# Moving a handful of vector pieces by half a step to two steps in a software-pipelined FFT-mixing and SiLU kernel

## Chip, cores and metric

One core of a Trainium2 chip. The metric is the device time of one execution in microseconds (us); medians of several runs are given. Engines are named as in the profile: PE is TensorE, PEld its weight loads, DVE is VectorE, ACT is ScalarE, POOL is GpSimd, SP is the engine whose queue issues most transfers.

## The reference

```python
def _attn_ref(x, filt_r, filt_i):            # x: 8 x 3008 x 256
    X = np.fft.rfft(x, axis=1)
    F = (filt_r + 1j * filt_i)[None, :, :]
    return np.fft.irfft(X * F, n=x.shape[1], axis=1).astype(np.float32)

def _moe_ref(x, w_in, w_out):                # x: 24064 x 256, d_ff 2048
    h = x @ w_in
    g = h * (1.0 / (1.0 + np.exp(-h)))
    return (g @ w_out).astype(np.float32)
```

The second function is applied to the result of the first, its 8 batches joined to 24064 rows.

## The kernel before

The FFT of a batch is done as small matrix products in stages ("spectral" work: `sums`, `stage1`, `forward`, `multiply`, `add`, `inverse`, `stage3`). The two large products with SiLU between them use a two-by-two block scheme with 7 products in place of 8 (`hidden`, `project`). A batch takes 48 steps of the large products, one pair of token blocks every 8 steps; while batch b runs, the spectral work of batch b+1 is slipped between its products. A step has 8 rounds. Every spectral piece is put at a step and a round, and all pieces are emitted in that order, so their place in each engine's program is fixed by hand (excerpts; "..." marks cuts, the notes behind # are added):

```python
def put(step, rnd, piece, *args):
    pending.append((step + rnd / ROUNDS, len(pending), lambda: piece(*args)))

def plan(b, part):
    at = STEPS * b                                       # STEPS = 48
    put(at - 49, 0, part["load_x"], 0)
    put(at - 49, 0, part["load_x"], 1)
    for u in range(8):
        put(at + u - 48, 5, part["sums"], u)
        put(at + u - 47, 3, part["stage1"], u)
    ...
    for g in range(NG):                                  # NG = 6 groups
        put(at + 3 * g - 37, 3, part["forward"], g)
        put(at + 3 * g - 37, 5, part["multiply"], g, 0)
        put(at + 3 * g - 36, 1, part["multiply"], g, 1)
        put(at + 3 * g - 36, 5, part["add"], g, 0)
        put(at + 3 * g - 35, 1, part["add"], g, 1)
        put(at + 3 * g - 35, 3, part["inverse"], g)
    put(at - 18, 5, part["load_t4"], 0)
    for g, step in enumerate((-16, -12, -8, -4)):        # stage3: waits for the t4 loads
        ...

stores = (((10, 1), (10, 5)), ((19, 5), (20, 1)), ((28, 5), (29, 1)), ((34, 1), (34, 5)),
          ((42, 1), (42, 5)), ((50, 1), (51, 1)))
for pair in range(len(pairs)):
    pending.append((NJP * pair - 2 + (5 if pair % per == 3 else 1) / ROUNDS, 100,
                    lambda pair=pair: tokens(pair)))
    for chunk in range(2):
        step, rnd = stores[pair % per][chunk]
        pending.append((pair // per * STEPS + step + rnd / ROUNDS, 99 + chunk,
                        lambda pair=pair, chunk=chunk: output(pair, chunk)))
pending.sort(key=lambda p: p[:2])
```

The second entry of a pending piece breaks ties, the smaller one first: a spectral piece has its number in the list, an output chunk 99 or 100.

The part of a step that the spectral pieces must not disturb (`pyz` is a bank of PSUM, the memory that the matmuls here write to, with one buffer; `combine` an elementwise operation):

```python
mm(xo, A11, yt[:, 0, 0:n], True)                         # round 0
...
mm(zo, A12, yt[:, 1, 0:n], True)                         # round 1: overwrites pyz
combine(v, g[:, 0, 0:n], zo, sums[:, 0, 0:n], ALU.add)
finish()                                                 # two subtractions of the step before
...
combine(v, g[:, 2, 0:n], yo, sums[:, 2, 0:n], ALU.add)   # round 4
...
mm(yo, S4, yt[:, 1, n:2 * n], False)                     # round 7: adds to pyz
combine(v, g[:, 1, 0:n], yo, sums[:, 1, 0:n], ALU.add)   # the last read of pyz
```

VectorE's other work: `sums` adds and subtracts two halves of an x tile, `multiply` and `add` are the complex product with the filter, `tokens` forms three differences for a new pair, `drain` copies accumulators out every 8 steps, `output` transposes results before they are stored. POOL adds up the drained blocks (s<-s).

## Time and profile before

| | before |
|---|---|
| runs, us | 2782.37, 2777.46, 2782.92; with three later ones, median 2780.23 |
| PE busy | 96% of 2777.8 us |
| DVE, ACT, POOL busy | 60%, 40%, 18% |
| one batch of 48 steps, steady | 331.24 us |
| PE's waits for DVE's g, as listed | 11.1 us, 17 times |

How to read it: PE is the bound, so what counts is not how busy VectorE is but whether it hands over in time. All losses below are taken from the starts of successive matmuls (0.216 us apart for one record of 256 columns), since the profile models their ends. A step is timed from the start of its round-0 product to that of the next step.

### The profile page before, as it was taken

To read this page: it belongs to the slowest core of one execution; us is meant where nothing else is said; L and a number is where in the kernel's file an instruction comes from. 1 tells how busy PE (TensorE), PEld (TensorE's weight loads), DVE (VectorE), ACT (ScalarE), POOL (GpSimd) and SP (SyncE) were. 2 spreads that over 40 slices of the span, in tenths; PEclk is the share of its full clock that TensorE was granted. 3 is DMA by queue.
4 is the path that set the end of the run, shared out by engine and by line. 5 is a ranking of instruction groups with operands and counts; after the bars stand their busy time and mean duration, and the time that the engine had idled before them with its cause. 6 is when DMAs were issued, how large, how long until landed. Compare 5 with 4: busy or idle time off the path is not lost.

```text
span 2777.8 us, 39564 instructions
## 1 busy us (share of the span) xinstructions
PE 2670.7 (96%) x14592; PEld 2253.3 (81%) x14592; DVE 1657.2 (60%) x3492; ACT 1098.0 (40%) x2994; POOL 505.1 (18%) x738
## 2 busy tenths in 40 slices
PE   3599999999999999999999999999999999999998
PEld 0368889788887888888897888978888788898987
DVE  3676655666556665566656665566655666555555
ACT  1244344433444334443444434443344433444443
POOL 2531310211111111111211121022111211010100
PEclk9799999999999999999999999999999999999999
DMA  9643211321114220232112311133111421110000
GB/s 188 182 121 74 54 40 30 94 71 39 46 39 104 61 51 20 71 84 65 35 38 76 80 47 42 37 82 84 39 46 31 105 63 44 31 25 22 9 15 15
DMA packets 186849, 166.56 MB, mean 60 GB/s; under 512 B 121120, under 2 KB 154528, under 8 KB 186400
## 3 DMA queue, kind: packets, MB, share of 16 engines
q1 hardware_dynamic: 164856, 111.90, 16.9%
q0 software_dynamic: 16256, 47.20, 6.8%
q10 hardware_dynamic: 5544, 4.93, 0.8%
q8 instruction: 114, 1.87, 0.3%
q14 instruction: 79, 0.65, 0.1%
HBM read 88.97 MB, written 74.97 MB: 59 GB/s over the span
## 4 chain that ended last, share of the span: by engine, by line
PE 91%; DVE 4%; DMA 3%; ACT 1%; issue 1%; POOL 0%; ACTq 0%; SPq 0%; DVEq 0%; POOLq 0%
PE acc L491 39%; PE px L435 24%; PE pyz L435 17%; PE pd L355 4%; PE pc L332 3%; PE pa L279 2%; PE pb L302 2%; DMA d<-t 1%; DVE g L406 1%; DVE u L267 1%; DMA t<-d 1%; DMA x<-in_x_dram 0%; DVE z L323 0%; DMA raw<-in_moe_w_out_dram 0%; DVE z L322 0%
## 5 line engine op out<-in xcount | busy, mean ns | idle before, releaser
L491 PE MATMUL acc<-g,w_t 128*128 128x256 f32 (+1 forms) x5376 | 1512.2, 375 | 0.4 <-DVE g L406 0.4
L491 PEld LDWEIGHTS acc<-g,w_t 128*128 128x128 f32 x5376 | 1021.8, 190 | 115.2 <-DVE g L406 0.8
L406 DVE TENSOR_TENSOR g<-pyz,abc 128x256 f32<-128x256 f32 (+1 forms) x1152 | 479.1, 416 | 609.9 <-ACT abc L456 351.9
L406 DVE TENSOR_TENSOR g<-g 128x256 f32<-128x256 f32 (+3 forms) x1152 | 612.4, 532 | 196.6 <-ACT g L439 183.5
L435 PE MATMUL px<-ty,w_t 128*128 128x256 f32 (+1 forms) x2304 | 693.8, 383 | 3.9 <-ACT abc L450 3.3
L439 ACT ACTIVATE g<-g 128x256 f32<-128x256 f32 (+1 forms) x1152 | 472.8, 410 | 243.1 <-DVE g L406 240.6
L435 PEld LDWEIGHTS px<-ty,w_t 128*128 128x128 f32 x2304 | 418.8, 190 | 130.3 <-issue 71.0
L435 PE MATMUL pyz<-y,w_t 128*128 128x256 f32 (+1 forms) x1536 | 454.4, 377 | 11.2 <-DVE g L406 11.1
L406 POOL TENSOR_TENSOR s<-s 128x256 f32<-128x256 f32 (+1 forms) x329 | 265.7, 825 | 1040.4 <-DVE s L509 520.1
L435 PEld LDWEIGHTS pyz<-y,w_t 128*128 128x128 f32 x1536 | 282.1, 189 | 58.1 <-DVE g L406 21.1
L450 ACT COPY abc<-px 128x256 f32<-128x256 f32 (+1 forms) x384 | 141.3, 368 | 373.9 <-PE px L435 373.9
L439 ACT ACTIVATE g<-px 128x256 f32<-128x256 f32 (+1 forms) x384 | 145.9, 380 | 300.8 <-PE px L435 300.8
L456 ACT COPY abc<-px 128x256 f32<-128x256 f32 (+1 forms) x384 | 142.8, 372 | 284.7 <-PE px L435 284.4
L340 POOL DMA_DIRECT2D d<-q x168 | 99.3, 597 | 728.1 <-DVE q L209 720.3
L435 PE MATMUL pyz<-ty,w_t 128*128 128x256 f32 (+1 forms) x768 | 226.4, 377 | 0.0
L435 PE MATMUL px<-y,w_t 128*128 128x256 f32 (+1 forms) x768 | 225.8, 376 | 0.0
L435 PEld LDWEIGHTS pyz<-ty,w_t 128*128 128x128 f32 x768 | 145.2, 190 | 18.8 <-DVE g L406 2.7
L435 PEld LDWEIGHTS px<-y,w_t 128*128 128x128 f32 x768 | 144.6, 190 | 18.1 <-ACT g L439 0.4
L355 PEld LDWEIGHTS pd<-wi_t,t 96*128 96x128 f32 x1024 | 130.6, 201 | 16.6 <-issue 13.9
L355 PE MATMUL pd<-wi_t,t 96*128 96x94 f32 x1024 | 129.5, 283 | 13.0 <-DMA t<-d 13.0
L443 ACT COPY abc<-px 128x256 f32<-128x256 f32 (+1 forms) x384 | 134.1, 349 | 0.1
L284 POOL DMA_DIRECT2D d<-t x128 | 65.5, 516 | 329.7 <-ACT abc L456 283.7
(49 smaller groups left out, 1320.0 us busy)
## 6 DMA issues: line engine op xcount, KB each, us to landing
d<-t POOLq DMA_DIRECT2D x128, 192.0 KB, 3.1
t<-d SPq DMA_DIRECT2D x96, 256.0 KB, 4.1
t<-d SPq DMA_DIRECT2D x64, 384.0 KB, 4.3
d<-q POOLq DMA_DIRECT2D x168, 128.0 KB, 2.7
out_dram<-o SPq DMA_DIRECT2D x636, 32.0 KB, 1.8
x<-in_x_dram SPq DMA_DIRECT2D x120, 128.0 KB, 3.1
x<-in_x_dram SPq DMA_DIRECT2D x120, 60.0 KB, 2.9
raw<-in_moe_w_in_dram SPq DMA_DIRECT2D x16, 256.0 KB, 5.3
```

The source lines that it names most:

```text
L279: nc.tensor.matmul(out=ps[h][64 * par:64 * par + 64], lhsT=wf_t[rows, par], rhs=ut[rows, par], start=True, stop=True)
L284: nc.gpsimd.dma_start(out=d1[par].rearrange("s p n c -> (s p) n c")[:, 4 * u:4 * u + 4, :], in_=t1[64 * par:64 * par + 2 * NS].rearrange(" ...
L332: nc.tensor.matmul(out=ps[i][:, k, :], lhsT=e_t[rows, g, k, ri, :], rhs=zs[k][rows, ri, :], start=(ri == 0), stop=(ri == 1))
L340: queue.dma_start(out=d2[a0:a0 + 2, :, :].rearrange("s n c -> n s c"), in_=qt[64 * p:64 * p + 64, :, :])
L355: nc.tensor.matmul(out=psv[:, i, :], lhsT=t4s[g][:, i, cb * 128:cb * 128 + 128], rhs=wi_t, start=True, stop=True)
L406: eng.tensor_tensor(out=out, in0=in0, in1=in1, op=op)
L435: nc.tensor.matmul(out=out, lhsT=w_t[:, c, 0, jp], rhs=rhs, start=start, stop=True, skip_group_check=True)
L439: nc.scalar.activation(out=g[:, k, 0:n], in_=g[:, k, 0:n] if src is None else src, func=AFT.Silu)
L443: nc.scalar.copy(out=sums[:, 0, 0:n], in_=xo)
L450: nc.scalar.copy(out=sums[:, 1, 0:n], in_=xo)
L456: nc.scalar.copy(out=sums[:, 2, 0:n], in_=xo)
L491: nc.tensor.matmul(out=acc[pair][i][:, h, 0:n], lhsT=w_t[:, c, 1, jp], rhs=g[:, k, 0:n], start=(jp == 0 and h == 0), stop=last, skip_group ...
```

## The change

The intent: VectorE has two drains in steps 0 and 24, and two pieces that stand in its queue beside them move elsewhere; the neighbours move to make room.

```diff
-        put(at - 49, 0, part["load_x"], 0)
-        put(at - 49, 0, part["load_x"], 1)
+        put(at - 51, 0, part["load_x"], 0)
+        put(at - 51, 0, part["load_x"], 1)
         for u in range(8):
-            put(at + u - 48, 5, part["sums"], u)
+            put(at + u - (48 if u else 49), 5, part["sums"], u)
...
-        for g in range(NG):
-            put(at + 3 * g - 37, 3, part["forward"], g)
...
-            put(at + 3 * g - 35, 3, part["inverse"], g)
+        for g, step in enumerate((-37, -34, -31, -28, -25, -21)):
+            late = 4 if g == 4 else 0
+            put(at + step, 3, part["forward"], g)
+            put(at + step, 5, part["multiply"], g, 0)
+            put(at + step + 1, 1, part["multiply"], g, 1)
+            put(at + step + 1, 5 + late, part["add"], g, 0)
+            put(at + step + 2, 1 + late, part["add"], g, 1)
+            put(at + step + (3 if late else 2), 3, part["inverse"], g)
...
-    stores = (((10, 1), (10, 5)), ((19, 5), (20, 1)), ((28, 5), (29, 1)), ((34, 1), (34, 5)),
+    stores = (((10, 1), (10, 5)), ((19, 5), (20, 1)), ((30, 1), (30, 5)), ((34, 1), (34, 5)),
```

Below, part 1 is the first sums and their loads, part 2 the fifth group's adds and inverse, part 3 the sixth group, part 4 the third pair's output.

More of the change, by code (lines that the diff above doesn't have):

```diff
@@ L380, in plan @@
         put(at - 39, 0, part["load_t2"], 1)
-        for g in range(NG):
-            put(at + 3 * g - 37, 3, part["forward"], g)
-            put(at + 3 * g - 37, 5, part["multiply"], g, 0)
-            put(at + 3 * g - 36, 1, part["multiply"], g, 1)
-            put(at + 3 * g - 36, 5, part["add"], g, 0)
-            put(at + 3 * g - 35, 1, part["add"], g, 1)
-            put(at + 3 * g - 35, 3, part["inverse"], g)
+        for g, step in enumerate((-37, -34, -31, -28, -25, -21)):
[6 more added lines that the diff above has]
+            put(at + step + (3 if late else 2), 3, part["inverse"], g)
         put(at - 18, 5, part["load_t4"], 0)
```

## The prediction

> **What bounds the kernel now.** I read the page first: busy shares, then the chain that ended last.
>
> ```profile
> PE 2670.7 (96%) x14592; PEld 2253.3 (81%) x14592; DVE 1657.2 (60%) x3492; ACT 1098.0 (40%) x2994; POOL 505.1 (18%) x738
> PE 91%; DVE 4%; DMA 3%; ACT 1%; issue 1%; POOL 0%; ACTq 0%; SPq 0%; DVEq 0%; POOLq 0%
> ```
>
> TensorE (PE) is the bound; VectorE (DVE), which the change rearranges, is busy 60% of the span. So only moments in which VectorE makes PE wait can be won. The list of waits, PE's own, longest first:
>
> ```profile
> PE pb L302 <- DMA t<-d: 27.3, 4, 21.2
> PE pa L279 <- DVE u_s L267: 16.1, 2, 10.8
> PE pd L355 <- DMA t<-d: 13.0, 2, 12.8
> PE pc L332 <- POOL z L322: 12.3, 4, 7.0
> PE pyz L435 <- DVE g L406: 11.1, 17, 1.0
> ```
>
> The first four (four waits or fewer each, up to 21 us) are start-up, before the loop of 384 steps (8 batches of 48), and the change leaves them alone. The fifth is in the loop: the second projection of a step writes the pyz bank and must wait until VectorE has read the previous step's last sum out of it.
>
> The "idle" of PE is smaller than the loss, because the ends of matmuls are modelled and overlap, so I went by starts in the timeline. In an unstalled step two records of one 256-column product start 0.216 us apart each, 0.43 us a product. The turn of a batch (steps 0 and 1), all engines:
>
> ```profile
> 1151.90 0.42 DVE L406 TENSOR_TENSOR g<-pyz,abc 128x256 f32<-128x256 f32 x1 [1.64 <-ACT abc L456]
> 1152.24 0.65 DVE L509 COPY s<-acc 128x480 f32<-128x480 f32 x1
> 1152.81 1.78 DVE L267 TENSOR_TENSOR u<-x 111x512 f32<-111x512 f32 x2
> 1153.04 3.98 POOL L406 TENSOR_TENSOR s<-s 128x240 f32<-128x240 f32 x4 [35.85 <-DVE s L509]
> ...
> 1153.73 0.59 PE L491 MATMUL acc<-g,w_t 128*128 128x256 f32 x2
> 1154.51 0.40 DVE L511 COPY s<-acc 128x240 f32<-128x240 f32 x1
> ...
> 1154.83 0.41 DVE L406 TENSOR_TENSOR g<-pyz,abc 128x256 f32<-128x256 f32 x1
> ...
> 1155.29 0.70 PE L435 MATMUL pyz<-y,w_t 128*128 128x256 f32 x2 [0.97 <-DVE g L406]
> ```
>
> The pyz product is due at 1153.73+0.43 = 1154.16 and starts at 1155.29: 1.13 us late, and its 0.70 instead of 0.59 is another 0.10. VectorE is the reason: in step 0 it has both the drain of the finished accumulators (0.65 and 0.40) and the x tile's two sums (u), and the g that frees the bank runs behind them. The same place at step 24 to 25:
>
> ```profile
> 1327.94 0.42 DVE L322 TENSOR_TENSOR z<-z,p 128x256 f32<-128x256 f32 x1
> 1328.28 0.92 DVE L323 TENSOR_TENSOR z<-z,p 128x256 f32<-128x256 f32 x1
> ...
> 1328.86 0.59 PE L491 MATMUL acc<-g,w_t 128*128 128x256 f32 x2
> ...
> 1329.90 0.70 PE L435 MATMUL pyz<-y,w_t 128*128 128x256 f32 x2 [0.44 <-DVE g L406]
> ```
>
> Due at 1329.29, started at 1329.90: 0.60 late plus 0.10. Here the first complex add of the fifth group (z) sits between the two drains.
>
> Last, how much room VectorE has in a step, from step 30:
>
> ```profile
> 1367.34 0.87 DVE L406 TENSOR_TENSOR g<-g 128x256 f32<-128x256 f32 x2
> 1368.13 0.68 DVE L406 TENSOR_TENSOR ty<-y 128x512 f32<-128x512 f32 x1
> 1368.85 0.89 DVE L406 TENSOR_TENSOR ty<-y,ty 128x256 f32<-128x256 f32 x2
> 1369.78 0.42 DVE L406 TENSOR_TENSOR g<-pyz,abc 128x256 f32<-128x256 f32 x1
> 1371.54 0.42 DVE L406 TENSOR_TENSOR g<-pyz,abc 128x256 f32<-128x256 f32 x1 [1.33 <-PE pyz L435]
> ```
>
> There are **two gaps**. The first, from the end of the finishing subtractions (1368.13) to the g that needs round 4 (1369.78), has 1.65 us; here the token differences fill it. The second, from 1370.12 to the last g at 1371.54, has about 1.4 us. The step takes 6.04 us. Pieces of round 1 land in the first gap, those of round 5 in the second.
>
> **What the Trainium skill says.** "SBUF — State Buffer", section "Who interferes with whom": a VectorE instruction with two SBUF inputs contends with a GpSimd instruction that reads SBUF, one blocking the other; with at most one SBUF input it does not. The trace agrees: z<-z,p takes 0.42 us alone and 0.92 beside the POOL sums s<-s, u<-x 0.68 and 1.18, while g<-pyz,abc (one input in PSUM) stays at 0.42. "Perfetto Trace Analysis", section "Tensor Engine Instruction (MATMUL, LD_WEIGHTS)": the end of a matmul is estimated from its size. The trace agrees, records last 0.37 to 0.38 us and start 0.216 apart, so stalls are read from starts. Same page, "Optimizing Scalar/DVE Operations": an engine that isn't saturated can still cause bubbles on others; that is what the two fences show.
>
> **The change part by part.** No instruction is added or removed; pieces move in VectorE's order (and a few loads in the queue's).
>
> 1. **First sums from step 0 to step 47** of the batch before; their x loads from step 47 to step 45. Gain: 1.13+0.10 = 1.24 us at each turn. I went through the turns: six (steady batches 1 to 6) show 1.13 to 1.14 with the 0.10. 6 x 1.24 = 7.4 us. Landing: step 47 has no piece and no drain, and no POOL work. Its steps are of 240 columns, 5.67 us, and the second gap runs from 1146.32 to the g at 1147.64, 1.3 us. Two sums start 0.60 apart and let the next start 0.60 later, 1.2 us. It fits: cost 0. The loads take about 3.1 us to land and have over two steps. At the start of the loop the sums of batch 1 now run before step 0, ahead of its first g: I estimate 1.2 us of delay to the chain of that cold step, of which 0.6 to 0.8 is got back, as step 0 then loses the sums before its last g (where PE now waits 0.47+0.10). Net cost about 0.4 us, once.
> 2. **Fifth group's adds by four rounds**: step 24 keeps one product pair (1.3 us, first gap) and the drains; the adds go into both gaps of step 25, the inverse from step 25 to 26. Gain: 0.60+0.10 in the six batches that show it (0, 2 to 6), 0.10+0.10 in batch 1: 6 x 0.70 + 0.2 = 4.4 us. Cost: POOL runs its sums until about 5.7 us into step 25, so the adds take some 0.9 us each. The finishing subtractions are slowed too (they end at 3.5 instead of 2.9 us). First pair: 3.5 to 5.1, so the round-4 g is 0.6 late, ending at about 5.55, and the product that overwrites its bank is due at 5.61: just in time. Second pair from 5.5, one of the two beside POOL: 0.56+0.33, done at 6.36 against 6.24 for the last g. At step 22 to 23 a last g that started 0.21 late cost PE 0.05+0.10. I allow 0.1 us in each of seven batches: 0.7 us.
> 3. **Sixth group a step later** (steps 27 to 29 for 26 to 28). Same pieces in steps of the same shape, no drain: 0. The t4 load that follows (round 5 of step 30) then waits for the inverse's writes, which leave POOL about 2.3 us after the evacuation and land 2.7 us later; it should be issued early in step 31, takes 4.3 us, and is wanted 3.45 us into step 32. Some 3.5 us to spare: 0.
> 4. **Third pair's output from steps 28/29 to 30**, both halves. It had to leave the adds of the sixth group. In step 30 it meets the token differences: first gap 0.7+1.6 = 2.3 us of work for 1.65, so the round-4 g slips by 0.65 and ends at 5.55 (limit 5.61 again); second gap 5.5 + 0.7 = 6.2 against 6.24. No stall by 0.05; I allow 0.1 us per batch for eight batches: 0.8 us (estimate).
>
> Sum: 7.4 + 4.4 - 0.4 - 0.7 - 0.8 = **9.9 us less**. From the median 2782.4: **2772.5 us**, 0.36%.
>
> **Rivals.** (a) *The stalls move*: steps 26 and 31 get a wait of 0.3 to 0.6 us instead of steps 1 and 25, because both gaps are filled to the edge there. For it: POOL's contention in step 25 and the 0.05 us margins. Against: by my sums above both places come out even or nearly so. If it holds, the gain is 4 to 6 us, giving 2777. (b) *The t4 load comes late*: the load now queues behind eight output transfers (about 0.5 us each) and PE waits at the first stage-3 piece in step 32; each microsecond late costs 7 us in all. Against: 3.5 us of slack. Then 2775 to 2790. (c) *VectorE isn't the cause* and the pyz waits are refilled by another wait (abc from ScalarE, accumulators): then the time stays at 2782. Against: in step 33, which has the drain alone, no stall is seen. (d) All margins hold and even the allowances go unspent: 2771.
>
> **Range and chances.** The three runs of before spread over 5.5 us (2777.5 to 2782.9), as large as half the gain, so the range is 2765 to 2779. Everything that the loop loses to waits of this kind is under 1% of the span, so faster by over 2% is out of reach (0.005). Slower by 2% would need 8 us per batch (0.005). Same: 0.99.
>
> **What would show it.** Right: at steps 1 and 25 the pyz product starts 0.43 us after the acc product before it; PE's wait for g falls from 11.1 us and 17 times to about 3 us; the u pair in step 47 takes 1.3 us, not 1.8; a batch takes 329.3 to 329.6 us instead of 331.24 (from one pc piece to the same one of the next batch, 1245.25 to 1576.49). Wrong: PE waits for g at steps 26, 31 or 0, for t at step 32, or the first steps take over 1 us longer. A gain under 4 us or over 13 us would make the prediction wrong.

## The result, and the profile after

| | before | after |
|---|---|---|
| median of 6 runs, us | 2780.23 | 2771.51 |
| lowest to highest | 2777.46 to 2782.92 | 2766.89 to 2773.52 |
| span profiled | 2777.8 | 2771.1 |
| steady batches 2 to 6 | 331.24 | 328.88 (two of them), 329.01, 329.33, 331.93 |
| steps 0 to 2 of the first batch | 24.74 | 27.65 |

The ratio is 0.9967, interval 0.9954 to 0.998: 0.3% faster. A ratio is the mean time of one kernel's fast runs over that of the other's of the same rounds, so not quite the ratio of the medians quoted.

PE's own list of waits after (cause: total us, times, longest us); "..." stands for lines left out:

```profile
PE pb L302 <- DMA t<-d: 24.9, 5, 17.8
...
PE pd L355 <- DMA t<-d: 13.7, 3, 12.3
...
PE pyz L437 <- DVE g L408: 2.9, 5, 0.8
```

The wait for g fell from 11.1 us to 2.9, and what is left is start-up. The line above it is less welcome: pd waited for DMA twice before, three times now.

The turn of the batch, timeline after (start, duration, engine, line, operation):

```profile
1145.84 1.28 DVE L267 TENSOR_TENSOR u<-x 111x512 f32<-111x512 f32 x2
...
1152.58 0.41 DVE L513 COPY s<-acc 128x240 f32<-128x240 f32 x1 [0.17 <-PE acc L493]
...
1153.01 0.42 DVE L408 TENSOR_TENSOR g<-pyz,abc 128x256 f32<-128x256 f32 x1
1153.24 0.59 PE L493 MATMUL acc<-g,w_t 128*128 128x256 f32 x2
...
1153.67 0.59 PE L437 MATMUL pyz<-y,w_t 128*128 128x256 f32 x2
```

The sums now run in step 47 and take 1.28 us, not 1.78, since POOL is idle there. The g that frees the bank runs at once behind the drain, and the pyz product starts 0.43 us after the acc product before it: no wait. Step 1 is 1.24 us shorter in each of batches 1 to 6.

Step 25 and the start of 26 after:

```profile
1330.10 0.91 DVE L322 TENSOR_TENSOR z<-z,p 128x256 f32<-128x256 f32 x1
...
1330.93 0.91 DVE L323 TENSOR_TENSOR z<-z,p 128x256 f32<-128x256 f32 x1
...
1331.77 0.41 DVE L408 TENSOR_TENSOR g<-pyz,abc 128x256 f32<-128x256 f32 x1
...
1332.32 0.61 PE L437 MATMUL pyz<-y,w_t 128*128 128x256 f32 x2
...
1332.97 0.42 DVE L408 TENSOR_TENSOR g<-pyz,abc 128x256 f32<-128x256 f32 x1
```

The adds beside POOL's sums take 0.91 us each, the round-4 g is 0.57 us later than in a free step (5.06 into the step against 4.49), and the S4 product behind it still starts when due, 5.61 into the step. The last g starts 0.20 us into step 26, as in a free step. Both gaps are full, and almost nothing spills over: about 0.02 us in this batch and five others, 0.14 us in batch 1, whose S4 product starts 0.04 us late with its second record another 0.10 us.

Step 30 after, where the output meets the token differences:

```profile
1367.50 0.42 DVE L408 TENSOR_TENSOR g<-pyz,abc 128x256 f32<-128x256 f32 x1
...
1367.83 0.76 DVE L523 STREAM_TRANSPOSE o<-s 128x256 f32<-128x256 f32 x2
...
1368.03 0.64 PE L437 MATMUL pyz<-y,w_t 128*128 128x256 f32 x2
```

Here it spills by a hair: 0.64 instead of 0.59, 0.05 us per batch (0.25 in batch 1, 0.11 in batch 6).

Step by step, the two profiles differ at these places only (us, after less before; first profile after and, in brackets, a second one taken later):

| where | batches | each | sum |
|---|---|---|---|
| steps 0 to 2, start-up | 0 | +2.90 (+2.64) | +2.90 |
| step 1 | 1 to 6 | -1.24 | -7.44 |
| steps 25 to 29 together | 0 and 2 to 6; 1 | -1.16; -0.49 | -7.45 |
| step 30 | 0 to 7 | +0.04 to +0.25 | +0.64 |
| step 32 | 1 to 6 | 0 to +3.04 (0 to +0.78) | +3.82 (+2.01) |

With +0.9 us from the part ahead of the loop, which varies by almost 4 us between all profiles, this is the 6.7 us between the spans. So the total came close to the predicted one, but three of its rows were not: steps 25 to 29 brought more, the start and step 32 cost more. The experiments are about those three.

### The profile page after: what moved, and what is told of

The parts are those of the page before. It is cut to its first block, busy times and chain, and to the rows that moved or that the text cites. A ratio compares the mean times of both kernels' runs of the same rounds, so it can differ in the third digit from the quotient of the medians.

```text
span 2771.1 us, 39564 instructions
## 1 busy us (share of the span) xinstructions
PE 2671.0 (96%) x14592; PEld 2258.3 (81%) x14592; DVE 1651.5 (60%) x3492; ACT 1100.0 (40%) x2994; POOL 501.1 (18%) x738
## 4 chain that ended last, share of the span: by engine, by line
PE 92%; DMA 3%; DVE 2%; issue 1%; ACT 1%; SPq 0%; ACTq 0%; POOL 0%; DVEq 0%; POOLq 0%
PE acc L493 40%; PE px L437 24%; PE pyz L437 17%; PE pd L355 4%; PE pc L332 3%; PE pa L279 2%; PE pb L302 2%; DMA d<-t 1%; DMA x<-in_x_dram 1%; DVE g L408 1%; DMA t<-d 0%; DVE u L267 0%; ACTq L340 0%; DMA raw<-in_moe_w_out_dram 0%; ACT work L577 0%
```

## The experiments

All ran correctly. "Before" is timed beside each. The diffs are against the changed kernel, except where said otherwise, and are cut down to what differs.

**Part 1 alone.** The first hunk of the diff on the kernel before.

```diff
-        put(at - 49, 0, part["load_x"], 0)
-        put(at - 49, 0, part["load_x"], 1)
+        put(at - 51, 0, part["load_x"], 0)
+        put(at - 51, 0, part["load_x"], 1)
-            put(at + u - 48, 5, part["sums"], u)
+            put(at + u - (48 if u else 49), 5, part["sums"], u)
```

> Part 1 alone: first sums in step 47, x loads in step 45, all else as before. My theory: at steps 1 of batches 1 to 6 the pyz product loses its 1.24 us wait (together 7.4 us), and the start of the loop gets longer by 2 to 3.5 us, as in the changed kernel (step 0 +2.5, step 1 +0.6), because the sums now stand ahead of the first g[...]. Steps 25 and 32 as before. Time 4 to 5.5 us under before. Rival (the longer start was chance of that one execution, or belongs to another part): the start is as before within 0.5 us and the time 7 us under before.

Measured: 2774.78 against 2780.31, ratio 0.998 (0.9965 to 0.9995). Step 1 lost 1.24 us in each of six batches, steps 0 to 2 grew by 1.97, nothing else moved. The theory holds for step 1. For the start it is not settled by this one profile, as the next run shows.

**Parts 2 to 4 alone.** The changed kernel, with sums and x loads as before.

```diff
-        put(at - 51, 0, part["load_x"], 0)
-        put(at - 51, 0, part["load_x"], 1)
+        put(at - 49, 0, part["load_x"], 0)
+        put(at - 49, 0, part["load_x"], 1)
-            put(at + u - (48 if u else 49), 5, part["sums"], u)
+            put(at + u - 48, 5, part["sums"], u)
```

> Parts 2 to 4 alone: sums and x loads back in steps 0 and 47. My theory: step 1 stalls again (1.13+0.10 in six batches), the start of the loop is as before; steps 25 to 29 together lose 1.16 us per batch as in the changed kernel (0.70 at the pyz product, 0.46 at the inverse product pc, which I had not counted), step 30 gains 0.05 and step 32 waits for the t4 load in some batches, 0 to 3 us each. Time 2 to 7 us under before, less steady from run to run than before. Rival (the waits of step 32 come from the x loads of part 1 in the same queue): no wait at step 32 here, 7.5 us under before.

Measured: 2777.55 against 2780.31, ratio 0.999 (0.9975 to 1.0005). Steps 25 to 29 lost 1.16 us a batch and step 32 waited in five batches (0.15 to 0.96 us), so the waits at step 32 do not come from the x loads. The start was not "as before": 1.63 us longer, with the sums in their old place. So a start that is longer by this much can come about without part 1. The two ratios together give about 0.997, the change's own.

**The second batch's sums back in step 0.**

```diff
-            put(at + u - (48 if u else 49), 5, part["sums"], u)
+            put(at + u - (48 if u or b == 1 else 49), 5, part["sums"], u)
```

> The changed kernel, but the sums of the second batch (the only ones that part 1 puts ahead of the loop) stay in step 0. My theory: steps 0 to 2 of the first batch are 2.9 us shorter than in the changed kernel's profile and as long as before (within 0.5 us); steps 1 and 25 of the later batches as in the changed kernel. Time about 2.5 us under the changed kernel, some 11.5 us under before. Rival (half clock in the first steps is chance): steps 0 to 2 stay long.

Measured: 2769.41 against 2780.31, ratio 0.9961 (0.9945 to 0.9978). That is too close to the change's 0.9967 to be told apart by time. Steps 0 to 2 took 25.25 us, 0.51 more than before and 2.4 less than in the first profile after. One profile is not enough here, because something else varies; the windows view shows it (stretch, its length, busy times and counts, then the granted clock of PE, DMA share, GB/s), first before, then after:

```profile
146.50:150.40 3.90, 3.79 (x9) 1.99 (x8) 2.54 (x6) 1.66 (x3) 0.00 (x0) 0.50 0.87 156
150.40:156.00 5.60, 4.11 (x16) 2.27 (x15) 4.65 (x8) 3.05 (x9) 1.87 (x2) 1.00 0.03 5
```

```profile
152.00:160.50 8.50, 7.40 (x16) 4.79 (x17) 4.09 (x10) 3.65 (x9) 1.42 (x2) 0.50 0.15 45
160.50:164.50 4.00, 4.00 (x22) 2.54 (x21) 3.57 (x8) 2.76 (x6) 0.37 (x1) 1.00 0.02 4
```

PE starts the loop at half clock in both; full clock came 3.9 us into it before and 13.2 us after. Over all 13 profiles, the 7 with the sums ahead of the loop took 26.69 to 27.65 us for steps 0 to 2 (mean 27.07), with full clock after 10.6 to 13.2 us; the 6 with the sums in step 0 took 24.74 to 26.39 (mean 25.46), with full clock after 3.9 to 11.9 us. The groups do not overlap; the difference of the means is 1.6 us. The start varies with the moment of full clock: with the sums in step 0 it took 24.74 and 24.75 us where full clock came after 3.9 and 4.2 us, but 26.37 and 26.39 us where it came after 11.9 and 11.8 us. So compare at nearly the same moment: the two profiles with the sums ahead whose full clock came after 12.0 us took 27.38 and 27.60 us, 1.0 to 1.2 us more than those last two. Step 0 was 1.2 and 1.6 us longer in them, and by the end of step 2 only 0.2 to 0.4 us of it had come back. These 1.0 to 1.2 us go with the sums' place at the same clock. Whether the sums ahead of the loop also delay the full clock stays open.

**The t4 load ahead of the output.**

```diff
-        put(at - 18, 5, part["load_t4"], 0)
+        put(at - 18, 0, part["load_t4"], 0)
```

> The changed kernel, but the first t4 load stands ahead of both output chunks of step 30 in the queue's order. My theory: the load waited behind all 16 output transfers and went out 11.5 to 12.8 us after the start of step 30; now it goes out 3 to 4.5 us after it, and PE never waits at the first pd product of step 32 (3.45 us into the step in every batch). Against the changed kernel's profile 3.8 us less, and runs agree more closely. Rival (the load is late because the inverse's writes are late): it goes out little sooner and step 32 still waits in some batches.

First the changed kernel in batch 4, the SP queue's timeline and then PE's (steps 30, 31 and 32 begin at 1691.30, 1697.38 and 1703.43):

```profile
1695.00 8.76 SPq L531 DMA_DIRECT2D out_dram<-o  x16
1704.09 0.79 SPq L345 DMA_DIRECT2D t<-d  x2
```

```profile
1708.21 2.00 PE L355 MATMUL pd<-wi_t,t 96*128 96x94 f32 x16 [1.16 <-DMA t<-d]
1710.04 0.98 PE L437 MATMUL px<-ty,w_t 128*128 128x256 f32 x2
```

The load goes out behind all 16 transfers, 12.8 us after the start of step 30. The output's second chunk and the load are put at the same round, and the tie goes to the output. Only in batch 0, whose load has the number 64, does it go to the load; the SP queue there, in the same profile (step 30 begins at 374.73):

```profile
378.43 3.67 SPq L531 DMA_DIRECT2D out_dram<-o  x8
382.42 0.32 SPq L345 DMA_DIRECT2D t<-d  x1
```

The load goes out behind eight transfers, 7.7 us into step 30, and step 32 of this batch has no wait in any run. In batch 4 PE waits 1.33 us by starts, and the next product takes 0.98 us (0.63 at the same place in the run below): the clock was at half for 3.4 us after the wait, which is why batch 4 lost 3.04 us and not 1.3. With the load moved, the same batch (its steps begin at 1689.06, 1695.15 and 1701.20):

```profile
1692.01 0.33 SPq L345 DMA_DIRECT2D t<-d  x1
1692.76 9.04 SPq L531 DMA_DIRECT2D out_dram<-o  x16
```

```profile
1704.65 1.92 PE L355 MATMUL pd<-wi_t,t 96*128 96x94 f32 x16
```

The load goes out 2.95 us into step 30, and pd starts 3.45 us into step 32 in all batches. Time 2766.65 against 2780.31, ratio 0.9951 (0.9937 to 0.9966). Of the 5.3 us between this span and that of the changed kernel, step 32 makes 3.8; the rest is start-up. The queue's order was the cause; the inverse's writes were there in time. Why batch 4 waits longest is open.

**The fifth group's adds back.**

```diff
-            late = 4 if g == 4 else 0
+            late = 0
```

> The changed kernel with the fifth group's adds and inverse back at their old rounds (adds in steps 24 and 25, inverse in step 25), sixth group and output as changed. My theory: step 25 has both its waits again, 0.60+0.10 at the pyz product and 0.46 at the first pc product, which stands behind the second adds; against the changed kernel +1.16 us per steady batch, about +7.5 us in all, some 2779. Rival (the 0.46 comes from the sixth group or the output, not from the adds): only +0.70 per batch, +4.5 us in all.

Measured: 2778.79 against 2780.32, ratio 0.9995 (0.998 to 1.0009). Step 25 was as long as before in every batch: 0.60 and 0.10 at pyz and the whole rest with them, though sixth group and output stayed moved. So part 2 brings all of the 1.16 us. (Step 32 cost 5.3 us in this execution, with one wait of 1.76 us followed by half clock.) What the 0.46 beyond the pyz wait is, the profile before shows in the list of waits of the weight loads and in PE's timeline of step 25:

```profile
PEld pc L332 <- DVE z L323: 3.7, 7, 0.5
```

```profile
1332.68 2.47 PE L332 MATMUL pc<-z,e_t 64*128 64x256 f32 x16
```

The inverse's 16 records took 2.47 us, where other inverses take 1.93 to 2.00: seven waits of about 0.5 us for the second adds, one a batch. They are booked on the weight load, so they are not in the matmuls' list that the prediction went by. The line did stand near the end of the unfiltered list that I had asked for first, and I passed over it. After the change no such line is left.

**The third pair's output back.**

```diff
-    ((30, 1), (30, 5))
+    ((28, 5), (29, 1))
```

> The changed kernel with the third pair's output back in steps 28 and 29, where it now meets the sixth group's adds. My theory: adds 0.75 and a chunk 0.74 make 1.5 us in the second gap of step 28 (1.4 us) and 1.5 us in the first gap of step 29 (1.65 us): a wait of at most 0.2 us at step 29; and the t4 load is issued early in step 30 again, so no wait at step 32. Time about 2767, under the changed kernel. Then moving the output was not needed and cost more than it brought. Rival (the output had to move): waits of 0.5 us or more per batch at steps 29 or 30, 2772 or above.

Measured: 2768.09 against 2780.32, ratio 0.9957 (0.994 to 0.9974). No wait at step 29, 30 or 32; steady batches took 328.82 to 328.84 us. Even the 0.2 us that I allowed did not appear. Part 4 was not needed: it cost the 0.05 us at step 30 and, through the queue, the waits at step 32.

**The sixth group back.**

```diff
-        for g, step in enumerate((-37, -34, -31, -28, -25, -21)):
+        for g, step in enumerate((-37, -34, -31, -28, -25, -22)):
```

> The changed kernel with the sixth group back a step earlier, so that its forward products stand right behind the fifth group's late inverse, in the same round of step 26. My theory: the forward products need the two PSUM banks that the inverse's results still hold; PE waits at the first pb of step 26 until both are copied out, 0.8 to 1.2 us in each of seven batches, so some 6 to 8 us over the changed kernel in batch lengths, less what step 32 gains by the earlier inverse. Rival (the sixth group moved only for VectorE's sake): no wait at pb in step 26, but waits for g at steps 27 to 29.

```profile
PE pb L302 <- DVE q L209: 5.4, 7, 0.8
```

Measured: 2775.85 against 2780.08, ratio 0.9987 (0.9972 to 1.0002), with the changed kernel at 0.9968 in the same rounds. One new line from the loop in PE's list: seven waits of 0.77 us at the forward product for the copy q, which empties the inverse's bank. Part 3 was needed, but for PSUM and not for VectorE. The size is just under what I expected.

**The changed kernel again.**

> The changed kernel once more, unaltered, beside two others. My theory: steps 1, 25 to 30 as in its first profile to 0.05 us; steps 0 to 2 together 1.9 to 2.9 us longer than before; step 32 waits in most of batches 1 to 6, longest in batch 4, by other amounts than the first time (0 to 3.5 us each). Time 2769 to 2774. Rival (the waits of step 32 were chance of one execution): none here.

Measured: 2770.24 against 2780.08, ratio 0.9968 (0.9952 to 0.9985). Step 32 waited in five batches, longest again in batch 4 (0.71 us by starts; 2.0 us in all). Steps 0 to 2 took 27.38 us.

**The faults mended.** Start kept, load first, and the third pair's chunks apart from the token differences:

```diff
-            put(at + u - (48 if u else 49), 5, part["sums"], u)
+            put(at + u - (48 if u or b == 1 else 49), 5, part["sums"], u)
-        put(at - 18, 5, part["load_t4"], 0)
+        put(at - 18, 0, part["load_t4"], 0)
-    ((30, 1), (30, 5))
+    ((30, 5), (31, 1))
```

> The changed kernel with three places altered: the second batch's first sums stay in step 0, the first t4 load goes ahead of the output chunks, and the third pair's two chunks go to the second gap of step 30 and the first gap of step 31, so that no gap has both them and the token differences. My theory: step 30 loses its 0.05 us, no wait at step 32, steady batches take 328.84 us, start-up about 1.5 us shorter than with the sums ahead (with a few tenths to 1.2 us of chance from the half clock). Time 2765, lower than any so far. Rival (gains overlap, the outputs now collide with something in step 31): a wait for g at step 31 or 32, and the time stays at 2767 or above.

Measured: 2766.39 against 2780.32, ratio 0.9953 (0.9938 to 0.9968). Batches 2 to 6 took 328.83 to 328.84 us, without a wait at steps 30 or 32. The time is 1.4 us above the 2765 that I named, and not told apart from that of the run with the load alone moved (ratio 0.9951).

**One more place, by the same rule.** The diff is against the run before this one.

```diff
-    NJP * pair - 2 + (5 if pair % per == 3 else 1) / ROUNDS
+    NJP * pair - (1 if pair % per == 3 else 2) + 1 / ROUNDS
```

> As the run called best, and also the fourth pair's token differences from the second gap of step 22 (1.5 us of work in 1.3 us of room; PE waits 0.05+0.10 at step 23 in every batch, before and after) to the first gap of step 23. Theory of the two gaps: that wait goes, 0.16 us in each of eight batches, 1.2 us under the run called best in its profile, and nothing else changes. Rival: the differences now come too late for step 24 or collide with the products there; then it is slower.

Measured: 2762.58 against 2780.32, ratio 0.9939 (0.9924 to 0.9954). Step 23 lost 0.16 us in all eight batches, and after start-up nothing else moved. In the profile before its pyz record pair was stretched, here it is not (PE's timeline of the two kernels, same place of the same batch):

```profile
1316.38 0.67 PE L435 MATMUL pyz<-y,w_t 128*128 128x240 f32 x2
```

```profile
1307.92 0.57 PE L437 MATMUL pyz<-y,w_t 128*128 128x240 f32 x2
```

The span is 3.9 us below that of the run before it, of which the moved differences explain 1.3; 3.0 us is the part ahead of the loop, which this edit does not touch (144.6 against 147.6 us, and 147.0 in the repeat below); steps 0 to 2 took 0.5 us more.

**The same version again.**

> The fastest version again, beside the changed kernel in the same rounds. Theory: all batches 1 to 6 take 328.7 to 328.8 us, no wait at steps 1, 23, 25, 30 and 32; 7 to 9 us under the changed kernel. Rival (its lead was one chip's luck): within 4 us of the changed kernel.

Measured: 2763.46 against 2780.08, ratio 0.9944 (0.9929 to 0.9958), beside 0.9968 for the changed kernel in the same rounds; 6.8 us between the medians, a little under the 7 to 9 expected. Batches 1 to 6 took 328.67 to 328.81 us. This version is the fastest.

## Why the prediction was right, and where its steps were not

The time was 2771.5 us for 2772.5 predicted, a gain of 8.7 us in the medians of 6 for 9.9. The mechanism was right: PE waited for the last read of the pyz bank, and the waits went when VectorE's pieces moved into free gaps. By its steps:

- **Part 1, 1.24 us at six turns, cost 0 in step 47**: as measured, 7.4 us. The pair of sums took 1.28 us there, as said.
- **"Net cost about 0.4 us, once"** at the start: mis-sized. It measured 1.6 us between the means of 7 and 6 profiles (2.9 in the profiled pair), and 1.0 to 1.2 at nearly the same moment of full clock. The delay of 1.2 us was about right; the 0.6 to 0.8 us "got back" was not, since only 0.2 to 0.4 came back. I also left out that PE ran at half clock there for a time that differs from run to run.
- **Part 2, "6 x 0.70 + 0.2 = 4.4 us"**: too small by 3.0 us. It measured 7.4 net, because the inverse's wait for the second adds (0.47 us in six batches, 0.43 in batch 1) was not in the sum. The line was among the waits of the weight loads; I went by the matmuls' list. Of the 0.7 us allowed for spilling over about 0.2 was spent, and the 7.4 has it taken off already.
- **Part 3, same pieces, 0**: right as a sum.
- **"It should be issued early in step 31 ... Some 3.5 us to spare: 0"** for the t4 load: this step failed. I put the load behind eight transfers, but it stood behind sixteen, as output chunks win a tie against it; in batches 1 to 6 it went out 11.5 to 12.8 us after the start of step 30 (7.7 in batch 0, where the tie went the other way), and PE lost 3.8 us in one execution and 2.0 in another. My rival (b) named this mechanism; the time stayed under the 2775 to 2790 us that I gave it, because the waits were short (0 to 1.3 us) and the gain of part 2 was larger than I had counted.
- **Part 4, 0.1 us per batch**: 0.64 us in all at step 30 for the 0.8 allowed. That it "had to leave the adds" was wrong, as the run with the output back shows.

The two errors of cost (1.2 to 2.5 us at the start, 2.0 to 3.8 at step 32) and the error of gain (3.0, and the allowance of 0.7) nearly cancel: that the total agrees to 1.2 us is in part luck. Two of the signs that I had named for being wrong did appear, the wait for t at step 32 and first steps over 1 us longer, and an undisturbed batch took 328.88 us, under the 329.3 to 329.6 named as a sign of being right. A total that agrees does not vouch for its terms.

Rival (a), stalls that move to steps 26 and 31, did not happen beyond 0.14 us (once) at the S4 product of step 25 and 0.05 us (0.11 and 0.25 once each) at that of step 30. Rival (c) did not happen. (d) fell with the t4 load.

## What to carry to other kernels

In a pipeline with fixed places, list each engine's free gaps within a step and fill them one piece at a time; by the counts used here, gaps filled to within 0.05 us at step 30 lost 0.05 us in most batches, and one overfilled by 0.2 us (step 22) lost 0.16. When an engine's piece moves, follow the transfers that it issues or precedes in the same queue, down to how ties are broken: that was the costliest oversight here, mended by one number. Read the waits of the weight loads together with those of the matmuls, and compare step by step rather than by totals.

## What the Trainium skill lacked or had wrong

- "TensorE: Matmul & The Clock Gate", Part 1, gives a free-running window of about 3.4 us and half clock after an idle window. The 3.4 us agree: half-clock stretches that ended inside a span lasted 3.41, 6.83, 10.24, 13.65 or 34.13 us, and the others too were whole multiples of 3.41. But waits of 1.33 and 1.76 us at step 32 were each followed by 3.41 us at half clock, while waits of 1.25 and 1.40 us at the same place were not. So half clock followed waits of well under a window in two of four cases, where the page speaks of a whole idle window; what decided between the cases is not shown.
- "Perfetto Trace Analysis" describes matmul and weight load in one timeline, and does not say that a wait can be booked on the weight load alone: 3.7 us in 7 waits for z were in that lane's list, none in the matmuls' list.
- No page that I read has the extra cost right after a wait: the first product's second record started 0.10 us late after the waits at steps 1, 23 and 25. It is not the waits' alone: after each inverse, without a wait, the next product's second record also started 0.32 us after its first, not 0.216.
- "SBUF — State Buffer", "Who interferes with whom", held: adds took 0.91 us beside POOL's sums and 0.42 alone. Its remark that the order of issue decides who blocks is not tested by these runs. They do show that both sides lost: at step 0, with the same shapes, POOL's seven sums took 6.29 us beside the two u sums (before) and 5.70 without them (after), and the u pair took 1.78 us beside them and 1.28 us away from them.
